# adaLN, attention and gMLP in fp32: the last head's products with V in threes, its first output product in one piece, one row tile's products moved ahead of transpositions

## The chip, the cores and the metric

The kernel runs on one core of one Trainium2 chip. The metric is the time of one execution on the device, in microseconds (us). TensorE (PE) multiplies, its weight loads (PEld) are listed apart; ScalarE (ACT), VectorE (DVE) and GpSimd (POOL) work element by element; SyncE (SP) issues most DMAs.

## The reference, cut to what matters

S = 2048 rows, D = 448 columns, H = 16 heads of 28, Fh = 896; everything is fp32.

```python
mod = (silu(c) @ w_mod)            # six rows: sa, ca, ga, sb, cb, gb
h = layernorm(x) * (1 + ca) + sa
q, k, v = split(h @ wqkv)          # 16 heads of 28
o = softmax(q @ k.T / sqrt(28)) @ v
x = x + ga * (o @ wo)
h = layernorm(x) * (1 + cb) + sb
z = gelu(h @ w_in); z1 = z[:, :896]; z2 = layernorm(z[:, 896:])
x = x + gb * ((z1 * (w_sp @ z2 + b_sp)) @ w_out)
```

The change touches the softmax attention of the last head, the product with `wo`, and the second layer norm with its transposition.

## The kernel before, in words

**Precision.** Most large products are made from fp32 operands split into two parts (high and low), so that one product becomes several: a row tile's output product (`wo_mm`, L827) has eleven of 448 columns, the list `STEPS`. The first nine of them, `STEPS_MAIN`, need only heads that are finished early; the last two, `STEPS_Z`, need the last heads too.

**Attention.** The loop at L975 runs over slots u from 0 to 256. Slot u stands for one head and one key tile of 128 keys: head u // 16, tile u % 16. In it PE makes four products of 128 x 512 with K, one for each group of 512 queries (`s_mm`, L738; the products are at L741, tile `st_ps`), ACT takes their exponentials (L745) into halves of a P tile, two halves a key tile. Between them stand four products that find the row maxima of a head 20 slots ahead (`m_mm`, L706; L709, tile `mt`), which DVE reduces at L714. That look-ahead is `LEAD` = 20, so from slot 236 on there are no such products. Every second slot PE multiplies the P of the two key tiles before with V (`pv_mm`, L751; L756, tile `o_ps`): four products of 32 columns a key tile, side by side in the array, each of them run as two instructions because its operands are plain fp32. They stand behind the slot's four products with K. P has six halves (`ppool`, 6 buffers of half a key tile's queries).

**Banks.** The tiles `st_ps`, `mt` and `wo_ps` are taken from seven PSUM banks (`banks`, L228); an eighth, `ps_o`, holds the running sum `o_ps`. Each engine works through its instructions in program order. Which of the seven a product gets is settled while the program is written, by a small planner, `First` (L921 on): it keeps an estimate of when each bank is free, in units of one product, and hands out the one that is free first. Products with V enter it as a pause:

```python
        def pause(self, n):
            self.t += 3.75 * n + 1.5
```

In its estimate an exponential starts every 2.1 units, a maximum every 2.6, and a bank is free 2.6 or 3.0 units behind the start. A bank given to `wo_ps` is held until the loop is over. Outside the loop the seven banks go round, the one used longest ago first.

**In the last head** one of the nine products of row tile 0 stands in each odd slot from 237 to 253, behind that slot's products with K. In slot 256 five products of row tile 1 stand ahead of the last two key tiles' products with V.

**Behind the loop** the last head's sums, reciprocal and scatter run while PE makes the output products of row tiles 1 to 7 (first nine, then the two of `STEPS_Z`), then whole row tiles (`wo_tile`: `wo_mm`, then `wo_add`, by which DVE adds the product to x at L1034 and so empties the bank). `h2_norm` (L1055, DVE) normalises a group of four row tiles; `h2_group` calls `ln_transpose` (L172 on): sixteen transpositions on PE (L179) into four banks, one for each 128 columns, then, column by column in the order 0, 2, 1, 3, ACT scales (L186, two buffers) and rounds (L193) and DVE subtracts (L150); the call `after(c)` follows a column's instructions. Row tile 13's products and its addition stand in that call for column 2 of group 0; row tile 15's in that for group 1. Behind them come the gate products (`z1_unit`, L1147).

**Memory and events.** The sums of blocks of w_sp that POOL forms in the loop use six buffers in `heapF` and six in `spool` (`ws_raw2`). Loads, additions and stores of these are called from a table of events by slot; the last store is called in slot 205. SP's and POOL's instructions come from this table as well.

Of the kernel before, what the change touches and what calls it, by code (L numbers as in the profile page):

```python
# [8 lines left out]
F32 = mybir.dt.float32  # L9
# [10 lines left out]
NT = S // 128  # L20
# [6 lines left out]
STEPS_MAIN = [(0, 0), (2, 2), (0, 3), (2, 5), (3, 0), (5, 2), (1, 1), (1, 4), (4, 1)]  # L27
STEPS_Z = [(6, 6), (6, 7)]
STEPS = STEPS_MAIN + STEPS_Z
# [70 lines left out]
def tile_adaln_mha_gmlp(ctx, tc, x, wqkv, wo, w_in, w_spT, b_sp, w_out, cT, w_mod0, w_mod, out):  # L100
# [33 lines left out]
    def hview(heap, off, a, b):  # L134
        return heap[:, off : off + a * b].rearrange("p (a b) -> p a b", b=b)
# [36 lines left out]
    def ln_transpose(xns, full_pool, dsts, scol, bcol, engs, los=(pool,) * 4, mid=None, after=None):  # L172

        tps = []
        for c in range(4):
            tp = bank("tp")
            tps.append(tp)
            for t in range(4):
                pe.transpose(tp[:, t * 128 : (t + 1) * 128], xns[t][:, c * 128 : (c + 1) * 128], ident)  # L179
        if mid:  # L180
            mid()
        for c in (0, 2, 1, 3):
            tp = tps[c]
            f = full_pool.tile([128, 512], F32, name="hfull")
            if engs[c] is act:
                act.activation(f, tp, AF.Identity, scale=scol[:, c : c + 1], bias=bcol[:, c : c + 1])  # L186
            else:
                engs[c].tensor_scalar(
                    out=f, in0=tp, scalar1=scol[:, c : c + 1], scalar2=bcol[:, c : c + 1], op0=ALU.mult, op1=ALU.add
                )  # L190
            hi = dsts[:, c if c < 3 else 6, :]
            if engs[c] is act:
                act.activation(hi, f, AF.Copy)  # L193
            else:
                engs[c].tensor_copy(hi, f)
            if c < 3:
                sub(los[c], dsts[:, 3 + c, :], f, hi)
            else:
                sub(los[c], hi[64:128], f[64:128], hi[64:128])
            if after:  # L200
                after(c)
# [7 lines left out]
    att = ctx.enter_context(ExitStack())  # L209
# [20 lines left out]
    def bank(name):  # L230
        k = mode[0](name) if mode[0] else banks[0]
        banks.remove(k)
        banks.append(k)
        return (ring_r if k < 3 else ring).tile([128, 512], F32, name=name, tag=f"b{k}")
# [453 lines left out]


    ppool = att.enter_context(tc.tile_pool(name="ppool", bufs=6))  # L690
    spool = att.enter_context(tc.tile_pool(name="spool", bufs=1))

    class Slots:

# [11 lines left out]
    def m_mm(j, kb):  # L706
        h, t = divmod(j, NT)
        mt = bank("mt")
        pe.matmul(  # L709
            mt, qst[h % 3][:, t * 128 : (t + 1) * 128], kst[h % 3][:, kb * 512 : (kb + 1) * 512], start=True, stop=True  # L710
        )
        if h not in pms:
            pms[h] = npool.tile([128, NT, 4], F32, name="pm")
        dve.tensor_reduce(out=pms[h][:, t, kb : kb + 1], in_=mt, axis=AX.X, op=ALU.max)  # L714
# [21 lines left out]
    ptiles = {}  # L736

    def s_mm(u, qb):  # L738
        h, kt = divmod(u, NT)
        st = bank("st_ps")  # L740
        pe.matmul(st, kst[h % 3][:, kt * 128 : (kt + 1) * 128], qst[h % 3][:, qb * 512 : (qb + 1) * 512], start=True, stop=True)  # L741
        if qb % 2 == 0:
            ptiles[u, -1] = ppool.tile([128, 2, 512], F32, name="P")
        p = ptiles[u, -1][:, qb % 2, :]
        act.activation(p, st, AF.Exp, scale=SCALE)  # L745
        ptiles[u, qb] = p
# [4 lines left out]
    def pv_mm(u):  # L751
        h, kt = divmod(u, NT)
        if kt == 0:
            otile[h] = ps_o.tile([128, 512], F32, name="o_ps", tag="o")
        for qb in range(4):
            pe.matmul(  # L756
                otile[h][32 * qb : 32 * qb + 32, :], V[:, kt, h, :], ptiles.pop((u, qb)), start=kt == 0, stop=kt == NT - 1
            )
# [68 lines left out]
    def wo_mm(t, steps):  # L827
        if t not in wo_ps:
            wo_ps[t] = bank("wo_ps") if t % 8 < 7 else ps_o.tile([128, 512], F32, name="wo_ps", tag="o")
        for a, b in steps:  # L830
            pe.matmul(
                wo_ps[t][:, :D],
                OT[:, a, t * 128 : (t + 1) * 128],
                wos[:, b, :],
                start=(a, b) == STEPS[0],
                stop=(a, b) == STEPS[-1],
            )
# [44 lines left out]
    LEAD = 20  # L882
    NU = H * NT
# [88 lines left out]
        )  # L972

    first_free = mode[0] = First()
    for u in range(NU + 1):  # L975
        for fn, a in events.pop(u, []):
            fn(*a)
        j = u + LEAD
        for qb in range(4 if u < NU else 0):
            s_mm(u, qb)  # L980
            if j < NU:
                m_mm(j, qb)
        if u % 2 and NU - LEAD < u < NU - 1:
            k = (u - NU + LEAD) // 2
            wo_mm(0, STEPS_MAIN[k : k + 1])
        if u == NU:
            wo_mm(1, STEPS_MAIN[:5])
        if u % 2 == 0 and u > 0:
            pv_mm(u - 2)
            pv_mm(u - 1)  # L990
            first_free.pause(2)
        for fn, a in late.pop(u, []):
            fn(*a)
    tail_events = {fn.__name__: [(fn, a)] for k in sorted(events) for fn, a in events[k]}
# [37 lines left out]
    def wo_add(t):  # L1032
        xt = x3[t]
        dve.tensor_tensor(out=xt[:, :D], in0=xt[:, :D], in1=wo_ps.pop(t)[:, :D], op=ALU.add)  # L1034
        sp.dma_start(x2_scr[t * 128 : (t + 1) * 128, :], xt[:, :D])
# [32 lines left out]
    def wo_tile(t):  # L1068
        wo_mm(t, STEPS)
        wo_add(t)  # L1070
# [64 lines left out]
    def h2_group(g, after=None):  # L1135
        if g >= 2:
            heaps.append(fh.tile([128, 4 * 896], F32R, name="heap", tag=("heapE", "heapC")[g - 2]))
            h2T.append(hview(heaps[-1], 0, 7, 512))
        xns = [x3.pop(4 * g + t) for t in range(4)]
        ln_transpose(xns, t3b, h2T[g], cols["cb"], cols["sb"], (act,) * 4, (dve,) * 4, None, after)  # L1140
# [15 lines left out]
    h2_norm(1)  # L1156
    wo_mm(12, STEPS)
    wo_add(12)
    h2_group(0, lambda c: wo_tile(13) if c == 2 else None)
    wo_tile(14)  # L1160

    def last_tile(c):
# [452 lines left out]
```

## Time and profile before

| | before |
|---|---|
| time, median of 3 runs | 1379.3 us (1378.1, 1379.3, 1380.59) |
| profiled execution | 1378.04 us |
| its span, first to last instruction | 1376.2 us |
| granted TensorE clock | 1.000 |
| busy: DVE, ACT, POOL | 1067.5, 805.1, 359.9 us |

A line of the profile's groups or timeline reads: start, duration, engine, line of the code, operation, tile written <- tiles read, form, and the count of instructions merged into the line. In square brackets stands how long the engine was idle before it, and what ended that. Products overlap in PE, so a product's duration (0.39 for 512 columns) is longer than the distance to the next. A figure with PEld is a weight load. "issue" as a releaser means that the profile shows nothing the engine waited for.

### The profile page before, as it was taken

The page shows a single profiled execution, that of the slowest core. Times are in us where ns is not written, and L with a number is a line of the kernel's source. Part 1 is how long each engine was busy: PE and PEld are TensorE (multiplying, and loading weights), DVE is VectorE, ACT ScalarE, POOL GpSimd, SP SyncE. Part 2 cuts the span into 40 slices and gives each one's busy share as a digit, 9 for nine tenths or more (in the row PEclk, how much of TensorE's full clock was granted, in tenths as well). Part 3 has the DMA queues.
Part 4 walks back from the last instruction along what each step waited for, and adds up shares of the span by engine and source line. Part 5 has one row for each costly group of instructions (what it writes and reads, how often), then busy time and mean ns, then how long its engine had stood idle before and what let it go on. Part 6 is the DMA issues. An engine that isn't in the chain of part 4 may idle for free.

```text
span 1376.2 us, 20532 instructions
## 1 busy us (share of the span) xinstructions
PE 1370.9 (100%) x7098; PEld 974.6 (71%) x7098; DVE 1067.5 (78%) x1688; ACT 805.1 (59%) x1472; POOL 359.9 (26%) x367
## 2 busy tenths in 40 slices
PE   9999999999999999999999999999999999999998
PEld 8888655555555555555555554888898888888898
DVE  7898888888888888888888880673367777999752
ACT  6623666676667666766677779464324544555420
POOL 2134335243624264645640002200011000000000
PEclk9999999999999999999999999999999999999999
DMA  8465757777667667777773110535604665788552
GB/s 292 138 172 180 226 143 228 201 220 206 230 197 229 188 226 238 231 207 232 231 218 101 37 44 23 174 142 190 216 16 152 223 202 187 248 281 269 181 174 98
DMA packets 137075, 254.28 MB, mean 185 GB/s; under 512 B 21832, under 2 KB 37322, under 8 KB 134426
## 3 DMA queue, kind: packets, MB, share of 16 engines
q1 hardware_dynamic: 134254, 248.79, 57.7%
q10 hardware_dynamic: 2718, 4.19, 0.9%
q8 instruction: 56, 0.92, 0.3%
q14 instruction: 47, 0.39, 0.1%
HBM read 174.53 MB, written 73.59 MB: 180 GB/s over the span
## 4 chain that ended last, share of the span: by engine, by line
PE 97%; DVE 2%; issue 0%; DMA 0%; ACTq 0%; ACT 0%; POOL 0%; DVEq 0%
PE st_ps L741 19%; PE o_ps L756 17%; PE mt L709 17%; PE z_ps L1373 5%; PE acc L1441 5%; PE acc L1442 5%; PE acc L1440 5%; PE pq L404 5%; PE z_ps L1147 5%; PE pv L386 2%; PE y_ps L1508 2%; PE y_ps L1509 2%; PE y_ps L1507 2%; PE acc L1449 1%; PE acc L1450 1%; PE acc L1448 1%
## 5 line engine op out<-in xcount | busy, mean ns | idle before, releaser
L714 DVE TENSOR_REDUCE pm<-mt 128x1 f32<-128x512 f32 x1024 | 630.6, 680 | 86.1 <-PE mt L709 86.1
L745 ACT ACTIVATE P<-st_ps 128x512 f32<-128x512 f32 x1024 | 515.4, 626 | 202.6 <-PE st_ps L741 201.8
L741 PE MATMUL st_ps<-qst,kst 128*128 128x512 f32 x1024 | 406.3, 406 | 0.0
L709 PE MATMUL mt<-kst,qst 128*128 128x512 f32 x1024 | 402.8, 393 | 0.0
L741 PEld LDWEIGHTS st_ps<-qst,kst 128*128 128x128 f32 x1024 | 191.6, 188 | 140.8 <-issue 93.0
L756 PE MATMUL o_ps<-P,V 128*32 128x512 f32 x2048 | 246.3, 599 | 0.0
L709 PEld LDWEIGHTS mt<-kst,qst 128*128 128x128 f32 x1024 | 192.7, 188 | 31.5
L869 POOL TENSOR_TENSOR ws_raw<-ws_raw 128x512 f32<-128x512 f32 x112 | 143.6, 1288 | 177.7 <-DMA ws_raw<-in_w_spT_dram 110.5
L1357 ACT ACTIVATE heapB<-raw_sp 128x512 fp32r<-128x512 f32 x156 | 96.7, 630 | 98.4 <-PE acc L1442 68.3
L756 PEld LDWEIGHTS o_ps<-P,V 128*32 128x32 f32 x2048 | 53.7, 109 | 122.8 <-issue 117.4
L1442 PE MATMUL acc<-heapB,heapA 128*128 128x512 f32 x312 | 121.5, 390 | 0.0
L1440 PE MATMUL acc<-heapB,heapA 128*128 128x512 f32 x312 | 121.5, 390 | 0.0
L150 DVE TENSOR_TENSOR heapB<-raw_sp,heapB 128x512 fp32r<-128x512 f32 x112 | 74.6, 686 | 28.0 <-ACT heapB L1357 27.8
L1441 PE MATMUL acc<-heapB,heapA 128*128 128x512 f32 x222 | 86.6, 390 | 0.0
L1440 PEld LDWEIGHTS acc<-heapB,heapA 128*128 128x128 f32 x312 | 58.6, 188 | 12.2
L1442 PEld LDWEIGHTS acc<-heapB,heapA 128*128 128x128 f32 x312 | 58.6, 188 | 12.0
L404 PE MATMUL pq<-heapD,heapD 128*128 128x512 f32 x196 | 61.9, 390 | 0.0
L150 POOL TENSOR_TENSOR ws_raw<-ws_raw 128x512 fp32r<-128x512 f32 x44 | 56.6, 1287 | 3.5
L785 POOL TENSOR_TENSOR osb<-osb,rb 128x512 f32<-128x512 f32 x15 | 19.2, 1280 | 112.0 <-DMA rb<-r_scr 93.3
L1441 PEld LDWEIGHTS acc<-heapB,heapA 128*128 128x128 f32 x222 | 41.7, 188 | 8.9 <-DVE heapB L150 0.3
L1376 ACT ACTIVATE z<-z_ps 128x448 f32<-128x448 f32 x32 | 17.4, 544 | 47.7 <-PE z_ps L1373 47.7
L170 POOL TENSOR_TENSOR rsz<-rsz,mhalf 128x1 f32<-128x1 f32 x16 | 14.3, 891 | 118.1 <-DVE rsz L169 118.1
(218 smaller groups left out, 1652.8 us busy)
## 6 DMA issues: line engine op xcount, KB each, us to landing
ws_raw<-in_w_spT_dram SPq DMA_DIRECT2D x136, 256.0 KB
ws_scr<-ws_raw SPq DMA_DIRECT2D x112, 256.0 KB
ws_raw<-ws_scr SPq DMA_DIRECT2D x88, 256.0 KB
raw_sp<-ws_scr SPq DMA_DIRECT2D x88, 256.0 KB
raw_sp<-in_w_spT_dram SPq DMA_DIRECT2D x68, 256.0 KB
wl_scr<-ws_raw SPq DMA_DIRECT2D x44, 256.0 KB
kst<-qk_scr SPq DMA_DIRECT2D x45, 224.0 KB
qst<-qk_scr SPq DMA_DIRECT2D x45, 224.0 KB
```

The source lines that it names most:

```text
L150: eng.tensor_tensor(out=dst, in0=a, in1=hi.bitcast(F32), op=ALU.subtract)
L404: pe.matmul(pq, wqk[:, b, m * 128 : (m + 1) * 128], hT[g][:, a, :], start=j == 0, stop=j == NST - 1)
L709: pe.matmul(mt, qst[h % 3][:, t * 128 : (t + 1) * 128], kst[h % 3][:, kb * 512 : (kb + 1) * 512], start=True, stop=True)
L714: dve.tensor_reduce(out=pms[h][:, t, kb : kb + 1], in_=mt, axis=AX.X, op=ALU.max)
L741: pe.matmul(st, kst[h % 3][:, kt * 128 : (kt + 1) * 128], qst[h % 3][:, qb * 512 : (qb + 1) * 512], start=True, stop=True)
L745: act.activation(p, st, AF.Exp, scale=SCALE)
L756: pe.matmul(otile[h][32 * qb : 32 * qb + 32, :], V[:, kt, h, :], ptiles.pop((u, qb)), start=kt == 0, stop=kt == NT - 1)
L869: pool.tensor_tensor(out=a, in0=a, in1=b, op=ALU.add if W_SUMS[v][2] > 0 else ALU.subtract)
L1357: act.activation(hi, raw[0], AF.Copy)
L1440: pe.matmul(o, zh[:, c], hi, start=p < 2 and kt == 0, stop=False, skip_group_check=p > 1)
L1441: pe.matmul(o, zh[:, c], lo, start=False, stop=False, skip_group_check=p > 1)
L1442: pe.matmul(o, zl[:, c], hi, start=False, stop=kt == 3, skip_group_check=p > 1)
```

## The change

In the last head the products with V come in groups of three key tiles: behind slots 243, 246, 249 and 252, then two in slot 254 and two in slot 256. Up to slot 240 they come in pairs as before. For this P gets three more halves: at slot 234 the pool of the weight sums, `spool`, is closed, and a pool `ppool2` of three is opened in its place; each third half comes from it. The nine products of row tile 0 no longer stand in the odd slots; all nine stand in slot 256, ahead of the five of row tile 1. In the second norm the eleven products of row tile 13 stand ahead of group 0's transpositions; its addition on DVE stays where it was.

```diff
     ppool = att.enter_context(tc.tile_pool(name="ppool", bufs=6))
-    spool = att.enter_context(tc.tile_pool(name="spool", bufs=1))
+    sums_s = att.enter_context(ExitStack())
+    spool = sums_s.enter_context(tc.tile_pool(name="spool", bufs=1))
+    p_pools = [(ppool, 6)]
...
         if qb % 2 == 0:
-            ptiles[u, -1] = ppool.tile([128, 2, 512], F32, name="P")
+            n = (2 * u + qb // 2) % sum(b for _, b in p_pools)
+            pool_, bufs = p_pools[1 if len(p_pools) > 1 and n % 3 == 2 else 0]
+            ptiles[u, -1] = pool_.tile([128, 2, 512], F32, name="P", bufs=bufs)
...
+    groups = {u: 2 for u in range(2, NU - NT + 1, 2)}
+    groups.update({u: 3 for u in range(NU - NT + 3, NU - 3, 3)})
+    groups.update({NU - 2: 2, NU: 2})
+    assert sum(groups.values()) == NU
     for u in range(NU + 1):
+        if u == NU - LEAD - 2:
+            sums_s.close()
+            p_pools.append((att.enter_context(tc.tile_pool(name="ppool2", bufs=3)), 3))
...
-        if u % 2 and NU - LEAD < u < NU - 1:
-            k = (u - NU + LEAD) // 2
-            wo_mm(0, STEPS_MAIN[k : k + 1])
         if u == NU:
+            wo_mm(0, STEPS_MAIN)
             wo_mm(1, STEPS_MAIN[:5])
-        if u % 2 == 0 and u > 0:
-            pv_mm(u - 2)
-            pv_mm(u - 1)
-            first_free.pause(2)
+        if u in groups:
+            for k in range(groups[u]):
+                pv_mm(u - groups[u] + k)
+            first_free.pause(groups[u])
...
     wo_mm(12, STEPS)
     wo_add(12)
-    h2_group(0, lambda c: wo_tile(13) if c == 2 else None)
+    wo_mm(13, STEPS)
+    h2_group(0, lambda c: wo_add(13) if c == 2 else None)
     wo_tile(14)
```

## The prediction

> **What bounds the kernel now.** I read the page first: the busy table and the chain.
>
> ```profile
> PE 1370.9 (100%) x7098; PEld 974.6 (71%) x7098; DVE 1067.5 (78%) x1688; ACT 805.1 (59%) x1472; POOL 359.9 (26%) x367
> ...
> PE 97%; DVE 2%; issue 0%; DMA 0%; ACTq 0%; ACT 0%; POOL 0%; DVEq 0%
> ```
>
> TensorE (PE) is busy all through and 97% of the chain is its own. So what matters is when each product starts: a microsecond by which the products of one stage start later is not recovered behind it. I then read the timeline of the last head, where no maxima are formed any more (from slot 236 on) and PE has only products with K (S below), products with V (PV below) and, one at each odd slot, an output product.
>
> ```profile
> 829.77 0.36 PE L831 MATMUL wo_ps<-heapD,heapD 128*128 128x448 f32 x1
> 829.96 1.08 PE L741 MATMUL st_ps<-qst,kst 128*128 128x512 f32 x4
> 830.98 1.93 PE L756 MATMUL o_ps<-P,V 128*32 128x512 f32 x16
> 832.83 1.19 PE L741 MATMUL st_ps<-qst,kst 128*128 128x512 f32 x4
> ```
> ```profile
> 850.32 0.37 PE L831 MATMUL wo_ps<-heapD,heapD 128*128 128x448 f32 x1
> 850.52 1.09 PE L741 MATMUL st_ps<-qst,kst 128*128 128x512 f32 x4
> 851.55 1.92 PE L756 MATMUL o_ps<-P,V 128*32 128x512 f32 x16
> 853.40 1.21 PE L741 MATMUL st_ps<-qst,kst 128*128 128x512 f32 x4
> ...
> 861.65 1.21 PE L741 MATMUL st_ps<-qst,kst 128*128 128x512 f32 x4
> 862.70 1.18 PE L831 MATMUL wo_ps<-heapD,heapD 128*128 128x448 f32 x5
> 863.81 1.92 PE L756 MATMUL o_ps<-P,V 128*32 128x512 f32 x16
> 865.66 0.68 PE L831 MATMUL wo_ps<-heapD,heapD 128*128 128x448 f32 x2
> ```
>
> The weight loads of one PV group (PEld), in a view of their own:
>
> ```profile
> 851.55 0.16 PEld L756 LDWEIGHTS o_ps<-P,V 128*32 128x32 f32 x8 [0.34 <-issue]
> 852.00 0.13 PEld L756 LDWEIGHTS o_ps<-P,V 128*32 128x32 f32 x4 [0.30 <-issue]
> 852.43 0.13 PEld L756 LDWEIGHTS o_ps<-P,V 128*32 128x32 f32 x4 [0.30 <-issue]
> ```
>
> The first row is slot 239's output product; slot 237 has one too. S of slot 241 starts at 832.83 and the last PV group ends at 865.66, so this stretch takes 32.83. Seven pairs run from 832.83 to 861.65: 4.12 a pair. A pair's PV takes 851.55 to 853.40, 1.85; within it the four-product passes follow each other at 0.43 to 0.45, two passes a key tile, so a third key tile adds 0.86. An output product takes 850.52 - 850.32 = 0.20; a pair without it, 3.92. Four S products behind an output product take 1.09, the last 0.40 of it, so they follow each other at 0.23; behind PV they take 1.21, so the first step is 0.34. The last S of a pair starts at 850.52 + 3 x 0.23 = 851.22, and PV 0.33 behind it.
>
> Then ACT, which takes the exponentials (exps):
>
> ```profile
> 145.82 5.98 ACT L745 ACTIVATE P<-st_ps 128x512 f32<-128x512 f32 x12
> ```
> ```profile
> 854.00 0.60 ACT L745 ACTIVATE P<-st_ps 128x512 f32<-128x512 f32 x1
> ```
> ```profile
> L745 ACT ACTIVATE P<-st_ps x12: 592/666/738, 145.8 to 151.1; 128x512 f32<-128x512 f32 x12
> ```
>
> Twelve in a row take 5.98, the last 0.74 of it: one starts every 0.477. Their recorded length grows through a run from 0.59 to 0.74. The first exp of a pair starts at 854.00, 0.60 behind its S product. Eight need 3.82, so ACT is fed by PE here, but by little.
>
> **The change, step by step: the last head.** Up to slot 240 only the two early output products (slots 237, 239) leave: -0.40. Their cover is nothing: PE has no idle time there.
>
> *Removed:* two changeovers between S and PV. A changeover costs 0.33 - 0.23 before PV, 1.85 - 4 x 0.43 = 0.13 at its end and 0.34 - 0.23 behind it, 0.34 in all: 0.68 at most.
>
> *Added:* twelve S products ahead of each PV group instead of eight, into seven banks (line 228). Count from the first S of a group. Exp k starts at 0.60 + 0.477(k - 1). S number 12 would start at 0.34 + 10 x 0.23 = 2.67; the banks go round by age, so it takes the bank of S number 5, whose exp starts at 2.51 and, 0.65 long, ends at 3.16. No S in this trace waits for an exp, so I bound that wait: nothing, if the bank is free before the exp's recorded end, or the whole difference. The nearest row is a transposition that waits for ACT to leave a bank:
>
> ```profile
> 899.73 0.78 ACT L186 ACTIVATE hfull<-tp,col_sb,col_cb 128x512 f32<-128x512 f32 x1 [3.18 <-DVE heapB L150]
> ...
> 900.55 0.20 PEld L179 LDWEIGHTS tp<-ident,x 128*128 128x128 f32 x2 [0.19 <-ACT hfull L186]
> ```
>
> It went on 0.05 behind ACT's recorded end (900.51). I take that: S 12 starts at 3.21, 0.54 late. And S itself has waited for a bank, for DVE, in the first head:
>
> ```profile
> 148.85 0.19 PEld L741 LDWEIGHTS st_ps<-qst,kst 128*128 128x128 f32 x1 [0.24 <-DVE pm L714]
> 148.85 0.50 PE L741 MATMUL st_ps<-qst,kst 128*128 128x512 f32 x1
> ...
> 149.19 0.40 PE L709 MATMUL mt<-kst,qst 128*128 128x512 f32 x1
> ```
>
> The product behind the waiting one came 0.34 later, not 0.23: a wait also costs 0.10 of restart. So PV starts at 3.21 + 0.33 + 0.10 = 3.64, takes 1.85 + 0.86 = 2.71, and the next S starts at 6.35. Queued behind the waiting S on PE is the PV group, and behind that the next S, for which ACT waits: its twelfth exp starts at 5.85 and would be followed at 6.32, but the next comes at 6.35 + 0.60 = 6.95. The wait feeds itself. PV's own need is met: its third key tile starts at about 3.64 + 1.74, and the last exp that it needs, number 8, starts at 3.94. Nor do the P buffers bind: nine halves hold four and a half key tiles, and a half is written again only behind the PV group that read it. Without any wait the group would be 2.67 + 0.33 + 2.71 = 5.71 by PE and 12 x 0.477 = 5.73 by ACT.
>
> The Trainium skill, Perfetto Trace Analysis, section Optimization Strategy, reads a gap that repeats on an engine that should be full as a sign of too few SBUF or PSUM buffers. By that rule the change buys the wrong buffer, P instead of banks, and the sum is the one above; no run here shows it for S yet.
>
> The Trainium skill, TensorE: Matmul & The Clock Gate, section Architectural detail: the array is 16× 32×32, not 1× 128×128, says that TensorE's queue pulls weight loads ahead of matmuls in flight. By that rule the restart would go, and the last head would cost 0.4 less; the PEld row at 148.85 disagrees, as the load starts only with its product, after 0.24 of idle time.
>
> *Moved:* nine output products to the end, 0.20 each. There they lie ahead of the last PV group, behind five that lie there already. The last exp starts at 861.65 + 0.60 + 3 x 0.477 = 863.68 and ends at 864.3, and its key tile's passes begin 852.43 - 851.55 = 0.88 behind the group's start, at 864.69: five products already cover it, so nine more hide nothing. The last slot goes from 4.01 to 5.83.
>
> Sum from 832.83: four groups of three 4 x 6.35 = 25.40, slots 253 and 254 as a pair 3.92, the last slot 5.83, together 35.15, against 32.83; less 0.40: **+1.9**. What follows (sums, reciprocal, scatter, output products) hangs on the end of the last PV group and moves with it. SP's and POOL's orders stay as they are; the three new P buffers lie where the weight sums' tiles were, whose last store is issued in slot 205, 29 slots ahead.
>
> **The second norm.** Rows of before:
>
> ```profile
> 892.63 0.49 PE L179 MATMUL tp<-ident,x 128*128 128x128 f32 x3
> 893.40 1.71 PE L179 MATMUL tp<-ident,x 128*128 128x128 f32 x13 [0.29 <-DVE x L1055]
> 894.99 4.73 PE L831 MATMUL wo_ps<-heapD,heapD 128*128 128x448 f32 x22
> 899.56 2.09 PE L179 MATMUL tp<-ident,x 128*128 128x128 f32 x16
> 901.41 1.67 PE L831 MATMUL wo_ps<-heapD,heapD 128*128 128x448 f32 x7
> ```
> ```profile
> 898.48 0.61 DVE L1034 TENSOR_TENSOR xl<-xl,wo_ps 128x448 f32<-128x448 f32 x1
> 899.01 1.28 DVE L150 TENSOR_TENSOR heapB<-hfull,heapB 128x512 fp32r<-128x512 f32 x2
> 900.21 0.61 DVE L1034 TENSOR_TENSOR xl<-xl,wo_ps 128x448 f32<-128x448 f32 x1
> ```
> ```profile
> 916.22 1.91 PE L179 MATMUL tp<-ident,x 128*128 128x128 f32 x16
> 917.88 0.48 PE L1147 MATMUL z_ps<-heapB,heapA 128*128 128x512 f32 x1
> ```
>
> Now row group 0's transpositions wait once for DVE's norm (892.63 to 893.40). With row tile 13's eleven products ahead (22 take 894.99 to 899.56, so 2.28) they start at 894.91 and run free, 1.66 as at 916.22, to 896.57; tile 14's products end at 898.85. But the banks go round by age too. Before, the requests are 12, four transposed columns, 13, 14, and group 1's columns take the banks of 12 and of group 0's columns. After, they are 12, 13, four columns, 14: group 1's second column takes the bank of **tile 13**. DVE empties it at the same place in its order as before, between the subtractions of group 0, at 900.21 to 900.82; nothing on DVE comes earlier, as it is busy with group 1's norm until 898.48. So twelve transpositions wait until 900.87, take 12/16 x 1.66 + 0.05 = 1.30, and tile 15's products start at 902.17 instead of 901.41: **+0.76**. Queued behind are these products and the first gate products; ACT, whose four columns of group 0 wait for DVE's subtractions, reaches group 1's no earlier than before. The gain hidden in it, about 0.5, is real and is eaten.
>
> **Sum.** +1.9 + 0.76 = +2.7. The profiled execution took 1378.04 (span 1376.2 and 1.8 around it), so 1380.7 of its own kind. It lies 1.3 below the median 1379.3 of the three runs (1378.1 to 1380.59), so I forecast 1382.0 as a median.
>
> **Rivals.**
> - *Banks do not bind.* If a bank is free 0.54 or more ahead of its exp's recorded end, S 12 never waits and ACT sets 5.73 a group: 4 x 5.73 + 3.92 + 5.83 - 0.40 - 32.83 = -0.6, with the second norm +0.2: 1379.5, not slower. For it: no S waits for an exp in this trace. Against: the transposition's row.
> - *The norm's wait is absent too* (if DVE had tile 13's addition earlier): about 0.5 at 893.40 and the 0.19 at 900.55 go instead, -0.7, and the total is -1.3: 1378.0. Against it: DVE's order at 900.21.
> - *The planner hands out banks out of age order: slower.* It picks by its own estimates (an exp every 2.1 of its units, a bank free 2.6 behind the exp's start, 3.75 a key tile of PV), not by these rows. If it puts S 12 on the bank of number 6, that S waits one exp longer, 0.49: 4 x 0.49 = 2.0 more, +4.7: 1384.0. It decides from one place out of order in each group. For it: twelve S in a row with no maxima between them is a pattern that before doesn't have. Against: in its estimates exps alone are served one behind the other, so banks come free by age.
> - *A waiting product's weights are loaded during the wait.* Then no restart is paid: 4 x 0.10 goes, +2.3: 1381.6. Against it: the weight load at 148.85.
>
> **How the numbers follow.** Chances: forecast 0.62, banks free 0.12, banks free and no norm wait 0.08, planner out of order 0.08, weights loaded early 0.10. A measurement tells about 0.2%, 2.76 us, from no change, and the forecast lies just inside, so I call it no change. With runs that spread by 1.2 either way, half of the forecast's cases and 0.3 of the last rival's lie beyond it, and all of the planner's: slower 0.31 + 0.03 + 0.08 = 0.42. Only spread could carry the second rival from -1.3 past -2.76, 0.3 of its cases: faster 0.02. Within: 0.56. The range takes in the forecast with its spread (1380.8 to 1383.4), reaches up to the planner's rival and down past the first one: 1379.2 to 1384.0.
>
> **What would show it.** In the profile after: S rows in the last head with idle time ended by ACT's exps, six to seven microseconds a group (6.35; 5.73 if banks don't bind); ACT's breaks about 0.6 a group; fourteen output products in a row ahead of the last PV group, and that group without a wait; 35 from S of slot 241 to the end of the last PV group; transpositions of group 1 that wait for an addition of DVE, and none of group 0 for its norm. I am wrong if groups take 5.7, or if the transpositions of group 1 run in 1.7.

## The result, and the profile after

The changed kernel takes 1386.01 us (median of six, 1382.16 to 1386.46) against 1378.76 of the kernel before (median of six): 7.25 apart. The ratio of the means is 1.0043, 95% interval 1.0029 to 1.0058, which is about 6 us. So the change makes the kernel slower, outside the range that ended at 1384.0. The profiled execution took 1386.46, the longest of the six, with a span of 1384.6.

The page of the changed kernel, the lines that answer to the two of before:

```profile
PE 1376.3 (99%) x7098; PEld 976.1 (70%) x7098; DVE 1068.3 (77%) x1688; ACT 804.8 (58%) x1472; POOL 359.9 (26%) x367
...
PE 29%; DMA 0%; ACT 0%; SPq 0%; issue 0%; DVE 0%; DVEq 0%
PE z_ps L1383 5%; PE acc L1450 5%; PE acc L1451 5%; PE acc L1452 5%; PE y_ps L1518 2%; PE y_ps L1517 2%; PE y_ps L1519 2%; PE acc L1458 1%; PE acc L1459 1%; PE acc L1460 1%; DMA wo_scr<-wout 0%; ACT z1t L1160 0%; SPq L1199 0%; SPq L1187 0%; DVE x2l L1522 0%
```

PE has the same 7098 products and is busy 5.4 longer in a span that is 8.4 longer. The chain tells more: 97% was PE's before; now it is followed back through PE for 29% only, some 400 us from the end, and there leaves PE for ACT (`z1t`), SP and the DMA of `wout`. So the place of interest lies near 980, in a stage that the diff doesn't touch.

I took the start of one PE product at each stage boundary from the two timelines: the last product of maxima (821.53 before, 821.98 after), the first product behind the last PV group (865.66, 868.04), the first gate product (903.73, 906.88), the first product of the second gate stage, `z2_gemm` (977.10, 982.52), and the first with w_sp (1048.44, 1056.88).

| stage | before | after | difference | forecast |
|---|---|---|---|---|
| last head, behind the maxima | 44.13 | 46.06 | +1.93 | +1.9 |
| output products, second norm | 38.07 | 38.84 | +0.77 | +0.76 |
| first gate stage to the start of the second | 73.37 | 75.64 | +2.27 | 0 |
| second gate stage | 71.34 | 74.36 | +3.02 | 0 |
| from there to the end | 327.8 | 327.7 | 0 | 0 |

The first two rows are the parts that were worked out, and they came as worked out. Five microseconds came in two rows that were forecast at nothing. The last 0.45 of the 8.4 lies ahead of these stages: the last product of maxima starts anywhere from 820.27 to 822.83 in the thirteen profiles.

The last head in the timeline of the changed kernel, PE:

```profile
832.88 3.76 PE L743 MATMUL st_ps<-qst,kst 128*128 128x512 f32 x12
836.56 2.78 PE L760 MATMUL o_ps<-P,V 128*32 128x512 f32 x24
839.27 3.71 PE L743 MATMUL st_ps<-qst,kst 128*128 128x512 f32 x12
842.91 2.78 PE L760 MATMUL o_ps<-P,V 128*32 128x512 f32 x24
845.62 3.70 PE L743 MATMUL st_ps<-qst,kst 128*128 128x512 f32 x12
...
862.21 1.20 PE L743 MATMUL st_ps<-qst,kst 128*128 128x512 f32 x4
863.25 3.01 PE L835 MATMUL wo_ps<-heapD,heapD 128*128 128x448 f32 x14
866.18 1.92 PE L760 MATMUL o_ps<-P,V 128*32 128x512 f32 x16
```

A group takes 845.62 - 839.27 = 6.35, the forecast's number. ACT's breaks between runs of twelve, and what the weight loads of S waited for, in two further views:

```profile
839.87 5.99 ACT L749 ACTIVATE P<-st_ps 128x512 f32<-128x512 f32 x12 [0.36 <-PE st_ps L743]
846.22 5.99 ACT L749 ACTIVATE P<-st_ps 128x512 f32<-128x512 f32 x12 [0.36 <-PE st_ps L743]
```
```profile
PEld st_ps L743 <- ACT P L749: 3.9, 14, 0.3
```

S waits for ACT 14 times, 3.9 in total, which never occurred before, and ACT waits for S once a group. Twelve exps at 0.477 take 5.73 of the 6.35, so about 0.6 is lost a group. The weight loads of the group that starts at 839.27, one by one, show which products wait:

```profile
841.50 0.19 PEld L743 LDWEIGHTS st_ps<-qst,kst 128*128 128x128 f32 x1 [0.30 <-ACT P L749]
841.98 0.19 PEld L743 LDWEIGHTS st_ps<-qst,kst 128*128 128x128 f32 x1 [0.30 <-ACT P L749]
842.47 0.19 PEld L743 LDWEIGHTS st_ps<-qst,kst 128*128 128x128 f32 x1 [0.30 <-ACT P L749]
```

These are numbers 10, 11 and 12. The forecast named only number 12, which starts at 842.47 - 839.27 = 3.20, against 3.21 forecast.

The second norm, PE and then DVE:

```profile
897.74 1.91 PE L179 MATMUL tp<-ident,x 128*128 128x128 f32 x16
899.41 2.48 PE L835 MATMUL wo_ps<-heapD,heapD 128*128 128x448 f32 x11
901.72 0.60 PE L179 MATMUL tp<-ident,x 128*128 128x128 f32 x4
903.28 1.53 PE L179 MATMUL tp<-ident,x 128*128 128x128 f32 x12 [0.96 <-DVE xl L1043]
904.57 2.48 PE L835 MATMUL wo_ps<-heapD,heapD 128*128 128x448 f32 x11
```
```profile
902.61 0.61 DVE L1043 TENSOR_TENSOR xl<-xl,wo_ps 128x448 f32<-128x448 f32 x1
```

The sixteen transpositions of group 0 run through; those of group 1 stop behind their first column until DVE has added tile 13 (902.61 + 0.61 = 903.22).

The start of the second gate stage, before and then after:

```profile
976.32 2.04 ACT L1151 ACTIVATE z1t<-z_ps 128x512 f32<-128x512 f32 x4
...
977.10 0.77 PE L1373 MATMUL z_ps<-heapD,heapB 128*128 128x448 f32 x3
```
```profile
979.73 0.62 DVE L1191 TENSOR_TENSOR raw_out<-raw_out,bc_gb 128x448 f32<-128x448 f32 x1 [3.16 <-DMA raw_out<-in_w_out_dram]
980.44 0.58 ACT L1193 ACTIVATE wout<-raw_out 128x448 fp32r<-128x448 f32 x1 [3.55 <-issue]
980.92 2.04 ACT L1160 ACTIVATE z1t<-z_ps 128x512 f32<-128x512 f32 x4
...
982.52 1.00 PE L1383 MATMUL z_ps<-heapD,heapB 128*128 128x448 f32 x3 [2.10 <-ACT z1t L1160]
```

In both, ACT is late with four gate tiles when PE comes to this stage, since in its queue a conversion for `w_out` (tile `wout`) stands ahead of them; its input is DVE's product, which waits for a load (after: DVE is done at 980.35, ACT starts at 980.44). Before, PE's first product starts while ACT is still on them. After, it starts at 982.52, when the third of the four is done (two steps of 0.48 behind 980.92, and its 0.58): its bank is that of the last gate unit but one. The reason is in the code, not in the stage: at L1391 (L1401 after) the order of the seven banks for this stage is written out by hand.

```python
    banks[:] = [5, 3, 6, 4, 0, 1, 2]
```

Followed through the code, the banks at this point, longest unused first, are 5, 1, 2, 6, 3, 0, 4 in the kernel before: the list begins with the oldest. In the changed kernel row tile 0 asks for its bank in slot 256 instead of slot 237, the rotation comes out as 2, 6, 3, 0, 4, 5, 1, and bank 5 is the newest but one.

What the wait brought with it, in stretches of the changed kernel (the column behind the busy times is the granted clock):

```profile
965.00:975.00 10.00, 10.00 (x46) 8.29 (x45) 3.52 (x5) 3.04 (x6) 0.00 (x0) 1.00 0.63 209
975.00:985.00 10.00, 7.90 (x32) 6.38 (x32) 2.13 (x4) 4.08 (x8) 0.00 (x0) 0.91 0.72 257
985.00:1000.00 15.00, 15.00 (x71) 13.62 (x70) 5.89 (x14) 3.27 (x6) 1.78 (x3) 0.95 0.67 226
```

Behind the idle time the clock is below 1: (1 - 0.91) x 10 + (1 - 0.95) x 15 = 1.7 lost. The rest of the second gate stage's +3.02 is a spacing of its products of 0.2067 instead of 0.2027, over 330 products 1.3.

### The profile page after: what moved, and what is told of

It is laid out like the page before. It is cut to its first block, busy times and chain, and to the rows that moved or that the text cites. A ratio compares the mean times of both kernels' runs of the same rounds, so it can differ in the third digit from the quotient of the medians.

```text
span 1384.6 us, 20542 instructions
## 1 busy us (share of the span) xinstructions
PE 1376.3 (99%) x7098; PEld 976.1 (70%) x7098; DVE 1068.3 (77%) x1688; ACT 804.8 (58%) x1472; POOL 359.9 (26%) x367
```

## The experiments

Ratios are of mean times, to the kernel before on the same chip, with 95% intervals. The theory, A: the stale list of banks makes PE wait, and what follows from the wait makes up the rest. The rival, B: the chain of loads, conversions and stores of `w_out` ran late by itself, and PE would have waited with any bank.

### The changed kernel with another list of banks

```diff
-    banks[:] = [5, 3, 6, 4, 0, 1, 2]
+    banks[:] = [6, 3, 5, 4, 0, 1, 2]
```

> The changed kernel with one list altered: the order in which the second gate stage takes the seven banks begins with the bank of the seventh-last but one gate unit (6, 3, 5, 4, 0, 1, 2) instead of the last but one (5, 3, 6, 4, 0, 1, 2). Theory A (the head's new rhythm leaves the banks in another physical order, so the written list begins with a bank that ACT has not emptied): PE's first product of that stage no longer waits (2.1 us in the changed kernel), the clock is not halved behind it, and what is left is the sum of the prediction, +2.7: a ratio of 1.0020, about 1381.5. Rival B (the chain of w_out loads, ACT and stores runs late by itself and PE waits for it whatever the bank): the wait of about 2 us and a time near 1386 stay, ratio 1.0045 to 1.0055.

The list now begins with bank 6, the oldest but one. The ratio is 1.0018 (1.0009 to 1.0027); by the medians, 1380.74 against 1377.96, +2.8. In its list of PE's waits the gate stage doesn't appear any more:

```profile
PE tp L179 <- DVE xl L1043: 1.2, 2, 1.1
PE wu L293 <- DVE ones L121: 1.0, 1, 1.0
```

The wait at the gate stage is gone, the clock stays full, the spacing is 0.2027, and the stages of the table read 46.07, 38.84, 73.38, 71.34. What is left is the forecast's +2.7. B falls, and not because the chain of `w_out` happened to be early here:

```profile
979.57 0.77 PE L1383 MATMUL z_ps<-heapD,heapB 128*128 128x448 f32 x3
980.59 0.58 ACT L1160 ACTIVATE z1t<-z_ps 128x512 f32<-128x512 f32 x1
```

ACT comes to its four tiles 1.02 behind PE's first product. In the profile after, it came to them 0.50 behind PE's arrival (980.92, and 982.52 - 2.10). The chain was later here, and PE didn't wait.

### The kernel before with a late bank first

```diff
-    banks[:] = [5, 3, 6, 4, 0, 1, 2]
+    banks[:] = [0, 3, 6, 4, 5, 1, 2]
```

> The kernel before with the second gate stage's list altered so that its first bank is that of the last gate unit but one (0, 3, 6, 4, 5, 1, 2), as it came out in the changed kernel; the head and the norm as before. Theory A: PE's first product of the stage waits for ACT, at least 0.7 us (ACT leaves that bank at about 977.9 by the trace of before, PE is there at 977.1), and up to 2 to 3 us where the chain of w_out loads is late; time up by 0.8 to 5, ratio 1.0006 to 1.0036. Rival B (the bank doesn't matter): ratio 1.0000.

1.0025 (1.0016 to 1.0034), with a wait of 1.7 for ACT:

```profile
980.19 0.87 PE L1373 MATMUL z_ps<-heapD,heapB 128*128 128x448 f32 x3 [1.72 <-ACT z1t L1151]
```

A list with another first bank, with head and norm untouched, costs over half of what the whole change costs. The clock stayed full behind the wait.

### The norm alone

```diff
-    h2_group(0, lambda c: wo_tile(13) if c == 2 else None)
+    wo_mm(13, STEPS)
+    h2_group(0, lambda c: wo_add(13) if c == 2 else None)
```

> The kernel before with the second part of the change alone: row tile 13's products ahead of group 0's transpositions, its addition where it was. By the prediction +0.76: the twelve transpositions of group 1 wait for DVE's addition of tile 13, ratio 1.0006. Rival (DVE's addition comes in time): -0.7, ratio 0.9995. The second gate stage starts without a wait in both.

1.0007 (0.9998 to 1.0015): by the times alone not to be told from none. By its profile the stretch from the last PV group to row tile 15's products is 36.54 against 35.74, +0.80, and PE's wait is there:

```profile
901.62 1.53 PE L179 MATMUL tp<-ident,x 128*128 128x128 f32 x12 [0.97 <-DVE xl L1034]
```

### The head alone, with the old list and with the other

The first kernel is the change without the lines of the norm; the second has, besides, the list 6, 3, 5, 4, 0, 1, 2.

> The kernel before with the first part alone: products with V in threes and the nine output products in slot 256; the norm as before. By the prediction's sum alone +1.9, ratio 1.0014. By theory A the stale list of banks adds its wait, so ratio 1.002 to 1.005, with a wait of PE for ACT at the start of the second gate stage. By rival B as much as the w_out chain is late in this program, wait or none.

> The first part of the change alone (threes, nine output products in slot 256), the norm as before, and the second gate stage's list as in the first experiment. Theory: the head's own cost, +1.9, and no wait at the gate stage: ratio 1.0014, against 1.0028 with the old list. Rival (the first part alone brings about another loss in that stage): above 1.002.

1.0028 (1.0017 to 1.0039) with the old list, 1.0012 (1.0003 to 1.0021) with the other. In both the last head takes 46.06. With the old list PE waits at the gate stage:

```profile
981.34 0.86 PE L1382 MATMUL z_ps<-heapD,heapB 128*128 128x448 f32 x3 [1.42 <-ACT z1t L1160]
```

So the list's cost belongs to the head's part, which moves the requests for banks, and the norm's part has none of it.

### The very last gate unit's bank first

```diff
-    banks[:] = [5, 3, 6, 4, 0, 1, 2]
+    banks[:] = [4, 3, 6, 0, 5, 1, 2]
```

> The kernel before with the second gate stage's list beginning with the bank of the very last gate unit (4, 3, 6, 0, 5, 1, 2). ACT leaves that bank one exponential-like step (0.48) later than the last but one, for which PE waited 1.7 us. Theory A (the length of the idle time decides): PE waits about 2.2, and as in the changed kernel (2.1 and more) the granted clock is halved for one stretch of 3.4 us behind it and the stage's products follow at 0.2067 instead of 0.2027: +2.7 for the wait and its start, +1.7 for the clock, +1.2 for the stage, ratio 1.003 to 1.0042. Rival (the halved clock of the changed kernel's profile has nothing to do with the wait): the wait alone, ratio 1.0020 to 1.0028, clock full, spacing 0.2027.

1.0023 (1.0013 to 1.0033), eight executions from 1378.65 to 1382.64; the profiled one is the slowest of them. It shows a wait of 2.63, and behind it what the changed kernel had:

```profile
965.00:975.00 10.00, 10.00 (x46) 8.28 (x45) 2.96 (x4) 3.62 (x7) 0.00 (x0) 1.00 0.59 188
975.00:985.00 10.00, 7.37 (x28) 6.24 (x27) 1.88 (x3) 3.06 (x6) 0.00 (x0) 0.83 0.62 228
985.00:1000.00 15.00, 15.00 (x75) 13.62 (x74) 6.87 (x16) 3.81 (x7) 2.44 (x3) 1.00 0.54 181
```

A clock of 0.83 over ten microseconds, 1.7 lost; the stage takes 74.36 as in the changed kernel, with a spacing of 0.2067. So the drop follows the wait, in a program whose head and norm are those of before. The ratio lies below theory A's 1.003 and inside the rival's 1.0020 to 1.0028. Shorter waits in the other executions would explain that, but only one was profiled, so it is not shown.

### The addition of tile 13 earlier

```diff
-    h2_group(0, lambda c: wo_tile(13) if c == 2 else None)
+    wo_tile(13)
+    h2_group(0)
```

> The kernel before with row tile 13's products ahead of group 0's transpositions, as in the change, but with DVE's addition for tile 13 directly behind that for tile 12, ahead of the subtractions. If the bank of tile 13 is what group 1's transpositions waited for, they run without a wait (16 in about 1.7) and the hidden wait for the norm (0.5) is saved too: tile 15's products start about 0.4 to 0.6 earlier than before, ratio 0.9996. Rival (group 1's transpositions wait for something else on DVE): as with the changed order, ratio 1.0006.

1.0007 (0.9998 to 1.0016), and row tile 15's products start 35.88 behind the last PV group, against 35.74: no gain. PE in this kernel:

```profile
894.33 1.91 PE L179 MATMUL tp<-ident,x 128*128 128x128 f32 x16
895.99 2.48 PE L831 MATMUL wo_ps<-heapD,heapD 128*128 128x448 f32 x11
898.31 1.47 PE L179 MATMUL tp<-ident,x 128*128 128x128 f32 x12
900.09 0.66 PE L179 MATMUL tp<-ident,x 128*128 128x128 f32 x4 [0.31 <-ACT hfull L186]
```

The wait for DVE is gone, but the fourth column now waits for ACT, whose buffers come free by DVE's subtractions, and these are one addition later. Neither theory had that. The output products ahead of group 0 were spaced at 0.2067 in this execution, so PE was about 0.5 late there; but it waits for ACT at 900.09 all the same, so this didn't set the result.

### Pairs, with the nine products at the end

```diff
-    groups = {u: 2 for u in range(2, NU - NT + 1, 2)}
-    groups.update({u: 3 for u in range(NU - NT + 3, NU - 3, 3)})
-    groups.update({NU - 2: 2, NU: 2})
+    groups = {u: 2 for u in range(2, NU + 1, 2)}
...
-    banks[:] = [5, 3, 6, 4, 0, 1, 2]
+    banks[:] = [6, 3, 5, 4, 0, 1, 2]
```

> The changed kernel with products with V in pairs throughout (nine halves of P, the nine output products in slot 256 as in the change), and the second gate stage's list as in the first experiment (6, 3, 5, 4, 0, 1, 2). Theory: the output products cost 0.20 each wherever they stand, so the head takes what it took before; what is left is the norm's +0.8: ratio 1.0006, against 1.0018 with threes. Rival (the piece at the end costs by itself, since in the odd slots the products were hidden in ACT's time): +1.8 more, ratio 1.0018 or above.

1.0007 (0.9998 to 1.0016). Its last head takes 44.16, against 44.13 before and 46.06 with threes; PE:

```profile
851.34 2.14 PE L743 MATMUL st_ps<-qst,kst 128*128 128x512 f32 x8
853.40 1.92 PE L760 MATMUL o_ps<-P,V 128*32 128x512 f32 x16
855.26 2.11 PE L743 MATMUL st_ps<-qst,kst 128*128 128x512 f32 x8
```

A pair without its output product takes 855.26 - 851.34 = 3.92. So the piece at the end costs nothing against the odd slots, and the head's whole +1.9 is the threes'.

### Threes on six banks

```diff
+        if u == NU - LEAD + 1:
+            wo_ps[0] = bank("wo_ps")
         if u == NU - LEAD - 2:
```

> The changed kernel with one of the seven banks held from slot 237 on (row tile 0's, without any of its products there), so that threes run on six banks. Theory (S waits for the bank of an exp five places back, then four): each group of three takes one exp step longer, 6.83 instead of 6.35, and the head +1.9 more; the second gate stage's list begins with the oldest bank again, so no wait there: ratio about 1.0032. Rival (the groups are paced by ACT or by the changeover, not by banks): 6.35 a group as before, ratio 1.0018.

1.0042 (1.0030 to 1.0055), with no wait at the gate stage. PE in its last head:

```profile
840.11 4.19 PE L743 MATMUL st_ps<-qst,kst 128*128 128x512 f32 x12
844.23 2.78 PE L760 MATMUL o_ps<-P,V 128*32 128x512 f32 x24
846.94 4.19 PE L743 MATMUL st_ps<-qst,kst 128*128 128x512 f32 x12
```

846.94 - 840.11 = 6.83 a group, as the theory had it: one bank less, one exp step more. The last head takes 48.27, 2.2 above 46.06; the theory had 1.9, and three pairs around the threes take about 0.1 more each. Banks set the pace of the threes. This kernel shows one thing more: it keeps the old list, 5, 3, 6, 4, 0, 1, 2, but asks for row tile 0's bank in slot 237 as before. Followed through the code, bank 5 is the oldest again, and PE doesn't wait. With pairs and the request in slot 256 (the experiment above) the order comes out as in the changed kernel. So the slot of that request turns the rotation, not the threes.

### Row tile 15's products ahead of transpositions too

```diff
-            wo_tile(15)
+            wo_add(15)
         h2_stats(2, ((0, 2, 1, 3).index(c),))
 
+    wo_mm(15, STEPS)
     h2_group(1, last_tile)
```

This is the kernel before with the norm's part of the change and these lines.

> The kernel before with row tile 13's products ahead of group 0's transpositions as in the change and, besides, row tile 15's ahead of group 1's, the additions on DVE where they were. If the transpositions of group 1 only came too early for the bank that DVE empties at 900.8, they now start at about 901.1 and run free in 1.7, and both waits are gone: the first gate product starts 0.9 earlier than before, ratio 0.9993. Rival (ACT and DVE set the start of the gate stage): the first gate product waits, ratio 1.0000 or above.

PE in its profile:

```profile
895.08 1.91 PE L179 MATMUL tp<-ident,x 128*128 128x128 f32 x16
896.74 4.70 PE L831 MATMUL wo_ps<-heapD,heapD 128*128 128x448 f32 x22
901.28 1.91 PE L179 MATMUL tp<-ident,x 128*128 128x128 f32 x16
902.95 3.22 PE L1147 MATMUL z_ps<-heapB,heapA 128*128 128x512 f32 x13
```

Both groups of transpositions run free, 1.67, and the first gate product starts 37.06 behind the last PV group against 38.07: 1.0 earlier, as expected. Yet the ratio is 0.9999 (0.9990 to 1.0008). The interval holds 0.9993 as well as no gain; the times can't tell a microsecond here, so this version isn't shown to beat the kernel before.

### The changed kernel once more

> The changed kernel once more, unaltered, beside the two others. Theory: PE waits 0.7 to 2.5 us for ACT at the start of the second gate stage, as late as the w_out chain is in that execution; where the wait is above 2, the clock is halved for 3.4 us behind it. Ratio 1.003 to 1.006, and 1.0015 to 1.0045 above the first of this call. Rival (its first profile was a chance): no wait, ratio 1.002.

1.0034 (1.0022 to 1.0047), five executions from 1382.38 to 1384.82. The profiled one (1382.8) waits 1.37 at the gate stage with the clock full and the spacing at 0.2027; head and norm as in the first profile (46.06, and 36.55 to row tile 15's products). The wait recurs; its length doesn't.

## Why the prediction was wrong, point by point

**The last head** was right in mechanism and size, though three products of a group wait, not S 12 alone; the last wait sets the time. What held was the period of 6.35 from S 12's wait for the bank of S 5, the 0.05 of handing over, the 0.10 of restart, and nine output products that cover nothing: 35.16 from S of slot 241 to the end of the last PV group (832.88 to 868.04), against 35.15 forecast. Pairs (3.92, no loss) and six banks (6.83) show that the cause is the count of banks. What the Trainium skill, Perfetto Trace Analysis, section Optimization Strategy, says of a gap that repeats holds here, and the six banks show it: the buffers missing were PSUM's. The rival in which waiting weights are loaded early would have given 6.25; it didn't occur.

**The second norm** was right: row tile 15's products start 36.52 to 36.55 behind the last PV group in all six profiles with this order, against 35.74, by the wait that was named. In three of them group 1's first column waits 0.2 for DVE as well, which the forecast left out; the longer wait behind it hides that. The gain of about 0.5 for group 0 was eaten, as forecast.

**The step that failed** is the sentence "What follows (sums, reciprocal, scatter, output products) hangs on the end of the last PV group and moves with it." It is true of the work named there. It is not true of the banks: row tile 0's request for a bank is part of what was moved, and by moving it from slot 237 to slot 256 the change turned the rotation that a list written by hand, 416 lines further down, takes for granted. The sum put the stages behind the norm at nothing; they took 5.3 more in the profile, 2.27 up to the start of the second gate stage and 3.02 in it. The prediction followed the rotation for the norm and asked of the planner whether it hands out banks by age; it didn't follow the rotation to its next use. The cost is shown by one edit in either direction: with the list adapted the changed kernel is at 1.0018, and with the list put wrong the kernel before is at 1.0025.

**How the cost comes to vary.** By the bank alone the wait would be about 0.8: before, the third of ACT's four tiles is done at 977.85, and PE is there at 977.10. In the first profile after, the four start 980.92 - 976.32 = 4.60 later, PE's first gate product only 906.88 - 903.73 = 3.15, so about 1.4 more. That comes from the chain of `w_out`: DVE's second multiplication waited for its load 2.1 before and 3.7 after. The two lines, of the kernel before and of the changed one:

```profile
946.76 0.62 DVE L1181 TENSOR_TENSOR raw_out<-raw_out,bc_gb 128x448 f32<-128x448 f32 x1 [2.11 <-DMA raw_out<-in_w_out_dram]
```
```profile
951.54 0.63 DVE L1191 TENSOR_TENSOR raw_out<-raw_out,bc_gb 128x448 f32<-128x448 f32 x1 [3.70 <-DMA raw_out<-in_w_out_dram]
```

So B held a part: the chain's lateness doesn't make the wait, since the first experiment has none, but sets how long it is: 1.4, 1.4, 1.7 and 2.1 in four profiles, and 2.6 in the one whose bank ACT leaves a step later. That the spread of the changed kernel's times, 1382.16 to 1386.46, is made by this and by the clock is likely from the two profiles at 1386.46 and 1382.8, but not shown for the executions that weren't profiled.

**The range and the chances.** The forecast's own terms would have put the time at the edge of what can be told from no change, where the first experiment lies (1.0018). The chance for slower, 0.42, had the planner's rival as its only new loss, and that rival looked for disorder inside the last head, where there was none, instead of behind it.

## What to carry to other kernels

Before an edit moves a request for a buffer, follow the rotation of that pool to its next fixed point, an order written by hand above all: the instruction count and every neighbouring stage may look the same while a later stage begins on the newest buffer. Where two engines share a ring of banks, a burst of products runs ahead of the slower engine only until it meets a bank that isn't empty yet; from there it goes at the slower engine's step. Here, with a product every 0.23, an exp every 0.477 and seven banks, that was at the tenth product: twelve in a group lost 0.6, eight lost nothing. Read the chain of the page first: where it leaves the bound engine is where the time went.

## What the runs showed of the hardware beyond that

At the second gate stage an idle time of PE of 2.1 or 2.6 (two profiles) was followed by a clock reduced for a loss of 1.7; idle times of 1.4 (twice) and 1.7 were not. The Trainium skill, TensorE: Matmul & The Clock Gate, section Why this matters for your kernels, warns of gaps above about 3 us; here less sufficed, and the measurement decides. Nor does the length of one idle time decide everywhere. In five profiles PE was idle for 0.16 to 0.56 between 6 and 9 us from the start, and the clock from 9 to 12 us was 0.50 to 0.76; in the repeat of the changed kernel it was idle for 0.85 there and the clock stayed full. What decides there stays open.

Products of 448 columns run at one of two spacings, 0.2027 or 0.2067, and keep it for a whole stage. The output products of the kernel before (22.05 for 108 on PE's line at 868.30, the last 0.37 of it) have the first; those of the changed kernel's first profile and of three experiments the second; the second gate stage had the second only behind the reduced clock. The second makes PE 0.5 later over the output products and 1.3 over the second gate stage. In the changed order the 0.5 doesn't reach the time, since DVE's addition of tile 13 sets the norm's end (36.53 with the second spacing, 36.55 with the first). What chooses between them stays open: the output products have no idle time ahead of them that would differ.
